# Turning a gate vector on VectorE before it is stored, and giving the two halves of a last tile a buffer each

## The chip, the core and the metric

The kernel runs on one core of a Trainium2 chip. Its engines work side by side, each through a queue of its own: TensorE (PE; its weight loads are listed apart as PEld), VectorE (DVE), ScalarE (ACT), GpSimd (POOL) and SyncE (SP), whose queue starts nearly all of this kernel's DMA transfers. They wait for each other by semaphores. The metric is the device time of one execution in microseconds (us); lower is better.

## What is computed

Two attention blocks work on the same x (2048 rows of 448 numbers), and a gate mixes them row by row:

```python
x = A_x
g = _sigmoid((x * gate_w).sum(-1, keepdims=True))
a = _A_ref(x, A_wqkv, A_wo)
b = _B_ref(x, B_wqkv, B_wo)
return g * a + (1 - g) * b
```

Both project x to queries, keys and values for 16 heads of 28 numbers, and multiply the heads' results by an output matrix. A lets each position see 8 positions, 2 apart (itself and those before it). B lets every position see all 2048 (softmax over the whole row). The change touches how `1 - g` is stored, and one of the projection's tiles.

## The kernel before, in words

Matmuls are done in split precision: an operand is rounded to a high part, the rest is kept as a low part, and three products are summed.

**Projection** (loop from line 476, about the first 254 us). There are 92 tiles: 28 for B's queries and keys, 16 for B's values, then 48 for A (16 each for queries, keys and values). From tile 10 on a tile is computed as two halves of the contraction, on the upper and the lower 64 rows of TensorE, into the two banks of a PSUM pair `PJ[n % 2]`. `add_halves` (line 380) then copies both banks to one SBUF tile `raw` in one ScalarE instruction (line 387), and GpSimd adds the two halves into a staging tile `ast` (line 388). Each staging tile takes two projected tiles and is then stored to DRAM by SyncE (line 401). Between the projection's matmuls run half matmuls of B's scores (line 148), of which VectorE takes the row maxima (line 170), four of them for every two tiles.

Tile 90, the last that goes through `PJ`, is copied otherwise: ScalarE copies one half (line 384) and VectorE the other (line 385), because the main stage needs that PSUM at once. Tile 91 is computed at the start of the main stage in another bank (`last_tile`, line 459) and stored from line 466.

**Buffers.** `raw`, `ast` and later the probability tiles `P` (written by the exponentials, line 1021), `ow` and `tw` all come from one pool, `pair`, with 8 buffers of 128x2x512 numbers. A tile that gets a buffer waits until everything that used it before is done, a store from it included. The main stage takes five `P` tiles from it with its first five exponentials and reuses these five to the end.

**Gate.** Two columns of the weights for A's queries give the gate's logits, which GpSimd gathers in `zt` (128 partitions x 16 columns; row 16 p + j of x stands in partition p, column j). At tile 64 ScalarE takes the exponentials, at tiles 66 and 68 VectorE the reciprocals: `g_t` holds g, `omg` holds 1 - g. At tile 70 SyncE stores `omg` to a DRAM vector `og_scr` (line 539), turned: column j, partition p goes to place 128 j + p. Sixteen small loads (line 938) bring it back in the main stage as `og`, in the layout in which B's sums stand. `omg` has another use before that: while it is still zero, it is the source of two stores that clear the margin before A's keys and values (line 515, at tile 16).

**Main stage** (from line 1031, to about 830 us). 16 units of 16 steps; a step has 12 score matmuls (line 1016), up to three matmuls of scores for the maxima of a later unit (line 148), two exponentials, and 8 matmuls with the values (line 982). A's part runs on GpSimd and VectorE meanwhile. The **output** product (line 862) follows.

The order of the work on each queue is the order of the program's lines as it is written out. On SyncE the gate store follows the staging store of tile 70 and stands ahead of the staging store of tile 71 and of the loads into `QP` (line 99, called from line 133). The maxima of a unit are turned (`max_turn`, line 198) and stored in four pieces of 32 columns (`max_store`, line 203) in the same way as the change does it for the gate.

Of the kernel before, what the change touches and what calls it, by code (L numbers as in the profile page):

```python
# [8 lines left out]
F32 = mybir.dt.float32  # L9
F32R = mybir.dt.float32r  # L10
AF = mybir.ActivationFunctionType
ALU = mybir.AluOpType
# [3 lines left out]
S, D, H, DH = 2048, 448, 16, 28  # L16
NB, NJ, NG = 4, 16, 4
# [8 lines left out]
def gated_mix_kernel(ctx: ExitStack, tc: tile.TileContext, xT, xn, gw, wA, wB, woAB, out):  # L26
    nc = tc.nc
# [12 lines left out]
    og_scr = dram.tile([S], F32, name="og_scr")  # L40
# [3 lines left out]
    cp = ctx.enter_context(tc.tile_pool(name="cp", bufs=1))  # L44
    sp = ctx.enter_context(tc.tile_pool(name="sp", bufs=2))
# [7 lines left out]
    PJ, PM = PS[0:2], PS[2:4]  # L53
# [8 lines left out]
    make_identity(nc, ident)  # L62
    V = cp.tile([128, NJ, H, 32], F32, name="V")
    g_t = cp.tile([128, NJ], F32, name="g_t")
    omg = cp.tile([128, NJ], F32, name="omg")
    zt = cp.tile([128, NJ], F32, name="zt")
    og = cp.tile([128, NB, 16], F32, name="og")

# [15 lines left out]
    def pair(name):  # L84
        return pp.tile([128, 2, 512], F32, tag="P", name=name)
# [124 lines left out]
    t0 = pair("t0")[:, 0, :]  # L210
    nc.vector.memset(t0, 0.0)  # L211
    nc.vector.memset(zt, 0.0)
    nc.vector.memset(omg, 0.0)

    def warm(n):
        for _ in range(n):
# [6 lines left out]
    if True:  # L223
# [30 lines left out]
        def split_x(nb):  # L254
            r, t = xst[:, nb, 0:3, :], xst[:, nb, 3, :]
            tail = xh[nb][:, 3, :]
            o, i = LOW[nb], HIGH[nb]
            for kt in (3, 0, 1, 2) if nb == 1 else range(4):
                if kt < 3:
                    split(xh[nb][:, kt, :], xl[nb][:, kt, :], r[:, kt, :])  # L260
                else:
                    nc.scalar.activation(tail[i], t[i], AF.Copy)
                    nc.vector.tensor_tensor(out=tail[o], in0=t[i], in1=tail[i].bitcast(F32), op=ALU.subtract)
# [3 lines left out]
        def load_w(wi, tails=(False, True)):  # L267
            src, cols = WSRC[wi]
            if wi not in wraw:
                wraw[wi] = raw3(), wp.tile([128, 450], F32, tag="wt", name="wt"), sum(c1 - c0 for c0, c1 in cols) + 2 * (wi == GATE)  # L270
            r, t, _ = wraw[wi]
            for tail in tails:
                o = 0
                for c0, c1 in cols:
                    e = o + c1 - c0
                    if tail:
                        both(t[:, o:e], src[384:448, c0:c1])
                    else:
                        nc.sync.dma_start(r[:, :, o:e], src[0:384, c0:c1].rearrange("(k p) c -> p k c", p=128))
                    o = e  # L280

                if wi == GATE:
                    if tail:
                        both(t[:, o:o + 2], gw[0:2, 384:448].rearrange("i p -> p i"))
                    else:
                        for kt in range(3):
                            nc.sync.dma_start(r[:, kt, o:o + 2],
                                              gw[0:2, 128 * kt:128 * kt + 128].rearrange("i p -> p i"))

        def split_w(wi, kts):  # L290
            if wi not in wsets:
                wsets[wi] = [wp.tile([128, 4, 450], F32R, tag=g, name=f"{g}{wi}") for g in ("wh", "wl")]
            wh, wl = wsets[wi]
            r, t, n = wraw[wi]
            for kt in kts:
                split(wh[:, kt, :n], wl[:, kt, :n], r[:, kt, :n] if kt < 3 else t[:, :n], nc.gpsimd)
# [24 lines left out]
        def project(n):  # L321
            if n == 0:
                for m, p in FIRST:
                    product(m, p, None, p == (0, 0, 0), p == (0, 1, 3))
            elif n > 1:
                for i, p in enumerate(ORDER):
                    product(n, p, None, i == 0, i == len(ORDER) - 1)
# [51 lines left out]

        def add_halves(n, dst, gate=None):  # L380
            raw = pair("raw")
            cols = D + 2 * (gate is not None)
            if n == len(tiles) - 2:
                nc.scalar.activation(raw[:, 0, 0:cols], PJ[n % 2][:, 0, 0:cols], AF.Copy)  # L384
                nc.vector.tensor_copy(raw[:, 1, 0:cols], PJ[n % 2][:, 1, 0:cols])  # L385
            else:
                nc.scalar.activation(raw[:, :, 0:cols], PJ[n % 2][:, :, 0:cols], AF.Copy)  # L387
            nc.gpsimd.tensor_tensor(out=dst, in0=raw[:, 0, 0:D].rearrange("p (c e) -> p c e", e=dst.shape[-1]),  # L388
                                    in1=raw[:, 1, 0:D].rearrange("p (c e) -> p c e", e=dst.shape[-1]), op=ALU.add)
            if gate is not None:  # L390
                nc.gpsimd.tensor_tensor(out=gate, in0=raw[:, 0, D:D + 1], in1=raw[:, 1, D:D + 1], op=ALU.add)

# [2 lines left out]
        def a_tile(n, i, j):  # L395
            k = j // 8
            if j % 2 == 0:
                stage[k] = pair("ast").rearrange("p a b -> p (a b)")[:, 0:896].rearrange("p (c j e) -> p c j e", c=8, j=2)
            add_halves(n, stage[k][:, :, j % 2, :], zt[:, j:j + 1] if tiles[n][0] == GATE else None)
            if j % 2 == 1:  # L400
                nc.sync.dma_start(a_own[i][:, :, j - 1:j + 1, :].rearrange("c p j e -> p c j e"), stage[k])
# [28 lines left out]
        r, t = xst[:, 0, 0:3, :], xst[:, 0, 3, :]  # L430
# [3 lines left out]
        for kt in range(3):  # L434
            if kt:
# [3 lines left out]
                                    op=ALU.subtract)  # L439
            nc.vector.tensor_tensor(out=wl0[:, kt, wa], in0=wr0[:, kt, 0:256], in1=wh0[:, kt, wa].bitcast(F32),  # L440
                                    op=ALU.subtract)
# [34 lines left out]
        for n, t in enumerate(tiles[:-1]):  # L476
            wi = t[0]
            for w in loads:
                if loads[w] == n:
                    load_w(w)  # L480
            for w in splits:
                i, k = (n - splits[w][0]) * splits[w][1], splits[w][1]
                if 0 <= i < 4:
                    split_w(w, range(i, i + k))
            if n in (3, 5):
                split_x((n + 1) // 2)
            if n < FULL:
                project(n)
            else:
                project_halves(n, [S1_START <= m < S1_START + 80 for m in (n, n + 1)])  # L490
            if t[1] == "qk":
                for m in {0: (), 1: (0, 1)}.get(n, (n,)):
                    qk_tile(m, *tiles[m][2:4])
            elif t[1] == "v":
                add_halves(n, V[:, t[2], :, 0:DH])
            else:
                a_tile(n, t[2], t[3])
            if n == 1:
                split_x(1)
            if n == 4:  # L500
                for t in QP[1]:
                    nc.scalar.activation(t, t0, AF.Copy)
            while fini and fini[0][0] <= n:
                fini.pop(0)[1]()
            if n == 2:
                load_w(1, (False,))
            if n == 3:
                load_qhi(0)
            if n in (3, 8):
                load_k(0, KH[0], qk_hi, slice(0, 1024) if n == 3 else slice(1024, S))  # L510
            if n == 3:
                load_w(1, (True,))
            if n == 16:
                for i in (1, 2):
                    nc.sync.dma_start(a_scr[i][:, 0:NJ, :].rearrange("c j e -> c (j e)").rearrange(
                        "c (a b) -> c a b", b=NJ), omg[0:8, None, :].to_broadcast([8, 56, NJ]))
            if n == 32:
                nc.gpsimd.memset(V[:, :, :, DH:], 1.0)
            if n == 22:
                load_k(1, KH[1], qk_hi)  # L520
            if n == 62:
                load_k(0, KL[0], qk_lo)
            if parts and parts[0][0] <= n:
                _, u, t = parts.pop(0)
                max_store(u, max_turn(t))
            if finished and n < len(tiles) - 3:
                u = finished.pop(0)
                parts.append((n + 3, u, max_parts(u)))
            if n == 64:
                gate = []  # L530
                for sgn, dst in ((-1.0, g_t), (1.0, omg)):
                    e = sp.tile([128, NJ], F32, name="ez")
                    nc.scalar.activation(e, zt, AF.Exp, scale=sgn)
                    nc.gpsimd.tensor_tensor(out=e, in0=e, in1=V[:, 0, :, DH], op=ALU.add)
                    gate.append((dst, e))
            if n in (66, 68):
                nc.vector.reciprocal(*gate.pop(0))
            if n == 70:
                nc.sync.dma_start(og_scr.rearrange("(j p) -> p j", j=NJ), omg)
            if n == 76:  # L540
                load_q(0)

# [186 lines left out]
    for c in range(8):  # L729
# [20 lines left out]
        n = 0  # L750
# [365 lines left out]
```

## Time and profile before

| | |
|---|---|
| three runs | 900.95, 901.16, 902.78 us (median 901.16) |
| profiled execution | 902.81 us, of which the span of the core's instructions is 901.0 us |
| TensorE busy | 893.7 us, 99% of the span |
| VectorE, ScalarE, GpSimd busy | 82%, 71%, 71% |
| mean granted TensorE clock | 0.998 of full speed |
| DMA | 104.51 MB, mean 116 GB/s |

Rows of a timeline have the start in us from the span's start, the duration, the engine, the line of the kernel, the operation, output <- inputs, shapes and a count of merged instructions; in brackets stands how long the engine was idle before, and what ended that. Rows of waits have the waiting engine, its instruction, what released it, the total, the count and the longest. A table of stretches has, for each stretch of the span, its length, the busy time of PE, PEld, DVE, ACT and POOL with the number of instructions, the granted TensorE clock, the DMA engines' busy share (over 1 where transfers overlap on an engine) and the GB/s. The ends of matmuls are modelled, so a busy TensorE is not always one at full speed.

### The profile page before, as it was taken

What the parts mean: (1) busy time and instruction counts of PE and PEld (TensorE: products, weight loads), DVE (VectorE), ACT (ScalarE), POOL (GpSimd) and SP (SyncE); (2) the same over time, 40 slices, a digit from 0 to 9 for tenths busy, and PEclk for the clock granted to TensorE, in tenths of its full rate; (3) what the DMA queues carried; (4) which work ended last, traced back from release to release, by engine and by line L of the source; (5) the groups of instructions that cost most, each with busy time, mean ns of one, the idle gap of its engine ahead of it and who ended that gap; (6) DMA issues with size and microseconds to landing.
All of it is one profiled execution on the core that took longest, in us unless ns stands there. A gap on an engine that the chain in (4) does not pass through costs nothing.

```text
span 901.0 us, 20505 instructions
## 1 busy us (share of the span) xinstructions
PE 893.7 (99%) x8311; PEld 534.3 (59%) x8311; DVE 739.9 (82%) x962; ACT 642.4 (71%) x765; POOL 638.5 (71%) x505
## 2 busy tenths in 40 slices
PE   9999999999999999999999999999999999999998
PEld 7889999998954444444444444444444444434997
DVE  6688999997979999999999999999999999832220
ACT  6456434343368888988988989889888898897220
POOL 1489846463449789999999999999999698501000
PEclk9999999999999999999999999999999999999999
DMA  8887403459373242225325342452130322347681
GB/s 267 276 260 192 144 12 84 138 141 95 100 227 107 88 130 53 62 60 147 85 52 143 88 111 47 105 131 73 51 63 20 94 43 56 96 90 199 184 270 52
DMA packets 115974, 104.51 MB, mean 116 GB/s; under 512 B 77176, under 2 KB 84216, under 8 KB 115096
## 3 DMA queue, kind: packets, MB, share of 16 engines
q1 hardware_dynamic: 115448, 102.42, 42.7%
q8 instruction: 65, 1.06, 0.5%
q10 hardware_dynamic: 432, 0.79, 0.2%
q14 instruction: 29, 0.24, 0.1%
HBM read 62.20 MB, written 40.96 MB: 114 GB/s over the span
## 4 chain that ended last, share of the span: by engine, by line
PE 99%; ACT 1%; issue 0%; DVE 0%; ACTq 0%
PE T L1016 31%; PE av L982 28%; PE r L319 15%; PE r L314 8%; PE T L862 8%; PE r L148 4%; PE T L148 4%; PE r L217 0%; ACT P L1021 0%; PE av L462 0%; ACT raw L387 0%; DVE raw L385 0%; ACT raw L384 0%; ACT onhi L919 0%; DVE t L211 0%
## 5 line engine op out<-in xcount | busy, mean ns | idle before, releaser
L1021 ACT ACTIVATE P<-T 128x1024 f32<-128x1024 f32 x512 | 496.9, 1023 | 60.5 <-PE T L1016 58.4
L154 DVE TENSOR_REDUCE MX<-T 128x1 f32<-128x512 f32 x470 | 442.1, 954 | 32.9 <-PE T L148 15.7
L982 PE MATMUL av<-P,V 128*32 128x512 f32 x2048 | 272.7, 605 | 0.0
L1016 PEld LDWEIGHTS T<-QH,KH 30*128 30x128 f32 x1024 | 92.1, 181 | 230.1 <-ACT P L1021 196.5
L148 PE MATMUL T<-KH,QP 28*128 28x512 f32 x704 | 220.0, 456 | 0.4 <-DVE raw L385 0.4
L170 DVE TENSOR_REDUCE MX<-r 128x2 f32<-128x1024 f32 x160 | 192.7, 1221 | 24.2 <-PE r L148 21.6
L1016 PE MATMUL T<-QH,KH 30*128 30x512 f32 x1024 | 212.0, 489 | 0.2 <-ACT P L1021 0.2
L1016 PE MATMUL T<-QH,KL 28*128 28x512 f32 x1024 | 186.8, 395 | 0.0
L1016 PE MATMUL T<-QL,KH 28*128 28x512 f32 x1024 | 184.6, 392 | 0.0
L637 POOL TENSOR_TENSOR prod<-qt,kt 128x896 f32<-128x896 f32 x64 | 135.3, 2115 | 6.4 <-DMA kt<-a_scr 6.3
L387 ACT ACTIVATE raw<-r 128x896 f32<-128x896 f32 (+1 forms) x62 | 57.0, 920 | 98.4 <-PE r L319 91.9
L148 PE MATMUL r<-KH,QP 64*128 64x512 f32 x320 | 108.3, 394 | 1.1 <-issue 1.1
L698 POOL TENSOR_TENSOR oat<-oat,prod 128x896 f32<-128x896 f32 x48 | 101.2, 2108 | 2.0
L148 PEld LDWEIGHTS T<-KH,QP 28*128 28x128 f32 x704 | 86.0, 181 | 27.5 <-ACT P L1021 19.1
L388 POOL TENSOR_TENSOR ast<-raw 128x448 f32<-128x448 f32 x47 | 54.2, 1155 | 60.6 <-ACT raw L387 54.4
L319 PE MATMUL r<-wh,xh 64*128 64x448 f32 (+1 forms) x504 | 96.2, 367 | 0.5 <-ACT raw L387 0.5
L693 POOL TENSOR_TENSOR prod<-vt,L 128x896 f32<-128x896 f32 x56 | 95.3, 1702 | 0.2
L1016 PEld LDWEIGHTS T<-QL,KH 28*128 28x128 f32 x1024 | 94.5, 185 | 0.0
L1016 PEld LDWEIGHTS T<-QH,KL 28*128 28x128 f32 x1024 | 93.3, 183 | 0.2
L982 PEld LDWEIGHTS av<-P,V 128*32 128x32 f32 x2048 | 40.3, 107 | 77.6 <-issue 65.3
L319 PE MATMUL r<-wl,xh 64*128 64x448 f32 (+1 forms) x441 | 75.7, 368 | 0.0
L319 PEld LDWEIGHTS r<-wh,xh 64*128 64x128 f32 x504 | 74.6, 187 | 1.2 <-ACT raw L387 0.8
(121 smaller groups left out, 1129.1 us busy)
## 6 DMA issues: line engine op xcount, KB each, us to landing
a_scr<-ast SPq DMA_DIRECT2D x24, 448.0 KB
qk_hi<-qkh SPq DMA_DIRECT2D x24, 256.0 KB
qk_lo<-qkh SPq DMA_DIRECT2D x24, 256.0 KB
rbc<-rs SPq DMA_DIRECT2D x64, 64.0 KB
QP<-qk_hi SPq DMA_DIRECT2D x64, 56.0 KB
KL<-qk_lo SPq DMA_DIRECT2D x16, 224.0 KB
QH<-qk_hi SPq DMA_DIRECT2D x64, 56.0 KB
QL<-qk_lo SPq DMA_DIRECT2D x64, 56.0 KB
```

Of the source, the lines that this page charges most:

```text
L148: nc.tensor.matmul(bank, qhis[u][h % 2][r, 128 * qs:128 * qs + 128], KH[u // NB % 3][r, 512 * kc:512 * kc + 512], start=True, stop=True)
L154: i = nc.vector.tensor_reduce(MX[:, n % NMX:n % NMX + k], bank, axis=X, op=ALU.max)
L170: nc.vector.tensor_reduce(m, PM[k], axis=X, op=ALU.max)
L314: nc.tensor.matmul(bank, ws[c][rows, k, t[4]:t[4] + 128], x, start=first, stop=last)
L319: nc.tensor.matmul(bank[:, 0:cols], x, ws[c][rows, k, 0:cols], start=first, stop=last)
L637: nc.gpsimd.tensor_tensor(out=p, in0=qt[c], in1=kvt["k", c % 2][:, HALO - DIL * w:HALO - DIL * w + NJ, :], op=ALU.mult)
L693: nc.gpsimd.tensor_tensor(out=dst.rearrange("p j (h d) -> p j h d", d=DH), in0=kvt["v", c % 2][:, HALO - DIL * w:HALO - DIL * w + NJ, :].r ...
L698: nc.gpsimd.tensor_tensor(out=ows[c % 2][:, :, 0:56] if w == W - 1 else oat[c], in0=oat[c], in1=oat[c, w], op=ALU.add)
L862: writes(bank, nc.tensor.matmul(bank[:, :D], src, wo[c][k], start=(first and k == ks[0] and i == 0), stop=(last and k == ks[-1] and i == 2)))
L982: nc.tensor.matmul(av[32 * h:32 * h + 32, :], V[:, kt, 4 * g + h, :], tiles_[h], start=(kt == 0), stop=(kt == NJ - 1), skip_group_check=True)
L1016: nc.tensor.matmul(bank[a], (KH[g % 3], KH[g % 3], KL[g % 2])[t][r, ks], (qh, ql, qh)[t][r, :], start=(t == 0), stop=(t == 2))
L1021: e = nc.scalar.activation(p, one if a == "2" else mine, AF.Exp, scale=SCALE).ins
```

## The change

`omg` becomes the first 16 columns of a wider tile `omt` (128x32), which is cleared whole. At tile 70 VectorE turns `omt` in blocks of 32x32 into a new tile `r`, and SyncE stores 16 rows of each of its four groups of 32 partitions: four transfers with rows of 32 numbers (128 bytes) that lie together in DRAM, in place of one transfer of single numbers. And the second half of tile 90 goes to a buffer of its own, a further tile from `pair`; GpSimd's sum then reads the two.

```diff
-    omg = cp.tile([128, NJ], F32, name="omg")
+    omt = cp.tile([128, 32], F32, name="omt")
+    omg = omt[:, 0:NJ]
...
-    nc.vector.memset(omg, 0.0)
+    nc.vector.memset(omt, 0.0)
...
         def add_halves(n, dst, gate=None):
             raw = pair("raw")
+            other = raw[:, 1, :]
             cols = D + 2 * (gate is not None)
             if n == len(tiles) - 2:
                 nc.scalar.activation(raw[:, 0, 0:cols], PJ[n % 2][:, 0, 0:cols], AF.Copy)
-                nc.vector.tensor_copy(raw[:, 1, 0:cols], PJ[n % 2][:, 1, 0:cols])
+                other = pair("raw")[:, 1, :]
+                nc.vector.tensor_copy(other[:, 0:cols], PJ[n % 2][:, 1, 0:cols])
...
-                                    in1=raw[:, 1, 0:D].rearrange("p (c e) -> p c e", e=dst.shape[-1]), op=ALU.add)
+                                    in1=other[:, 0:D].rearrange("p (c e) -> p c e", e=dst.shape[-1]), op=ALU.add)
...
             if n == 70:
-                nc.sync.dma_start(og_scr.rearrange("(j p) -> p j", j=NJ), omg)
+                r = sp.tile([128, 32], F32, name="omr")
+                nc.vector.transpose(r, omt)
+                for a in range(4):
+                    nc.sync.dma_start(og_scr.rearrange("(j p) -> j p", j=NJ)[:, 32 * a:32 * a + 32],
+                                      r[32 * a:32 * a + NJ, :])
```

## The prediction

> **What bounds the kernel now.** I read the page first: busy shares and the chain that ended last.
>
> ```profile
> span 901.0 us, 20505 instructions
> PE 893.7 (99%) x8311; PEld 534.3 (59%) x8311; DVE 739.9 (82%) x962; ACT 642.4 (71%) x765; POOL 638.5 (71%) x505
> PE 99%; ACT 1%; issue 0%; DVE 0%; ACTq 0%
> ```
>
> TensorE carries the chain almost alone. So an edit on DVE, ACT or the DMA queues is worth only what it takes out of TensorE's own stream: idle time, and time in which it runs slower than elsewhere. The waits of TensorE show the idle time, 3.7 us in all:
>
> ```profile
> PE r L217 <- DVE omg L213: 1.5, 1, 1.5
> PE r L148 <- issue: 1.1, 1, 1.1
> PE r L319 <- ACT raw L387: 0.5, 1, 0.5
> PE T L148 <- DVE raw L385: 0.4, 1, 0.4
> ```
>
> The last row names the copy that the change splits off. The second and third I looked up in the timeline, and they lie together, at 213 to 215 us, soon after the gate store. A table of stretches around that store, with its last three columns (granted clock, DMA share, GB/s), shows more than the waits do:
>
> ```profile
> 204.00:214.00 10.00, 8.95 (x84) 8.54 (x83) 7.12 (x7) 2.14 (x4) 3.64 (x4) 1.00 1.36 27
> 214.00:216.00 2.00, 1.53 (x11) 0.98 (x9) 1.26 (x2) 1.58 (x2) 0.59 (x1) 0.84 1.44 178
> 216.00:218.00 2.00, 2.00 (x14) 1.77 (x12) 2.00 (x3) 0.14 (x1) 1.65 (x2) 0.50 0.90 243
> 218.00:220.00 2.00, 2.00 (x20) 1.84 (x18) 1.00 (x2) 0.03 (x1) 0.00 (x0) 0.81 0.84 229
> 222.00:253.00 31.00, 31.00 (x300) 30.29 (x297) 27.55 (x23) 11.04 (x12) 13.67 (x13) 1.00 0.37 99
> ```
>
> From 204 to 214 us the DMA engines are full (share 1.36) and move 27 GB/s; in the quiet stage after 222 us they move 99 GB/s at a share of 0.37. At the end of that jam TensorE falters, and then runs at half clock. SyncE's queue tells what went in just before:
>
> ```profile
> 172.41 1.72 SPq L205 DMA_DIRECT2D nm<-nms  x4
> ...
> 200.41 0.53 SPq L539 DMA_DIRECT2D og_scr<-omg  x1
> 202.62 0.36 SPq L401 DMA_DIRECT2D a_scr<-ast  x1
> 203.62 6.23 SPq L99 DMA_DIRECT2D QP<-qk_hi  x4
> ```
>
> The gate store L539 puts 2048 numbers of 4 bytes where no two neighbours of a row lie together: 2048 pieces. Staging stores (L401) go on through the quiet stage after 222 us without a jam, so I put the jam down to L539.
>
> What it costs is read from ScalarE's copy L387, one per projected tile:
>
> ```profile
> 197.78 0.92 ACT L387 ACTIVATE raw<-r 128x896 f32<-128x896 f32 x1 [1.62 <-PE r L319]
> ...
> 208.29 0.92 ACT L387 ACTIVATE raw<-r 128x896 f32<-128x896 f32 x1 [1.32 <-PE r L319]
> 214.42 1.73 ACT L387 ACTIVATE raw<-r 128x896 f32<-128x896 f32 x2 [5.21 <-PE r L148]
> ...
> 222.48 0.92 ACT L387 ACTIVATE raw<-r 128x896 f32<-128x896 f32 x1 [1.59 <-PE r L319]
> ...
> 232.88 0.92 ACT L387 ACTIVATE raw<-r 128x896 f32<-128x896 f32 x1 [1.60 <-PE r L319]
> ```
>
> Four tiles before the jam take 208.29 - 197.78 = 10.51 us, four after it 232.88 - 222.48 = 10.40, the four across it 14.19. The jam costs 3.68 to 3.79 us; I take 3.74. The granted clock explains part: 2 us at 0.84, 0.50 and 0.81 lose 0.32 + 1.00 + 0.38 = 1.70 us. The other 2.04 are the two gaps (1.05 and 0.47 us) and weak filling around them.
>
> **The change, part by part.**
>
> *Gate store.* Removed: L539, one issue of 0.53 us and its 2048 pieces. Added: one VectorE transpose, four issues and 64 pieces of 128 bytes. Both have a twin in this kernel, the maxima's turn L200 and store L205, of the same 128x32 shape and 128-byte rows:
>
> ```profile
> L200 DVE STREAM_TRANSPOSE nms<-nmt x16: 199/202/219, 88.3 to 786.8; 128x32 f32<-128x32 f32 x16
> 172.40:174.40 2.00, 2.00 (x23) 2.00 (x21) 1.92 (x2) 0.21 (x2) 1.16 (x1) 1.00 0.64 181
> 197.31 2.36 DVE L170 TENSOR_REDUCE MX<-r 128x2 f32<-128x1024 f32 x2 [0.27 <-PE r L148]
> ```
>
> The transpose takes 0.20 us among the maxima near 198.5 us, where VectorE idles 0.27 us (197.31) and so holds it. Without it a maximum would be 0.20 late, and so would the next score half. Behind SyncE's new wait stand the four issues and the staging store at 202.62; the transpose is done before SyncE reaches it at 200.41, and four issues of L205's kind (1.72) end at 202.13, so nobody is moved. The twin's stretch (172.40 to 174.40) has TensorE full at clock 1.00: the new pieces cost TensorE nothing there. Their bounds: 0 below; above, the whole 3.74 if 128 bytes jam as 4 do. At the old jam's rate, 14 us (200.41 to 214.42) for 2048 pieces, 64 would take 0.44 us of DMA, off TensorE's path. I take 0, by the twin. The Trainium skill ("DMA: Bandwidth & Descriptors", Specifications) speaks against the edit: pieces under 512 bytes cause a read-modify-write, and 128 is still under. By that the new store stays of the slow kind and part of the 3.74 would be left; the twin's row disagrees, and the sum goes by it.
>
> How much of 3.74 leaves? The profile does not show the jam as releaser of TensorE: the rows name issue and ACT, and ACT in turn names TensorE. So the gain is bounded by 0 and 3.79. I take 3.74, because full DMA engines, falter and clock follow each other within one jam and nowhere else.
>
> *Memset L213* grows from 16 to 32 columns:
>
> ```profile
> 1.37 0.07 DVE L213 MEMSET omg<- 128x16 f32 x1
> 5.28 0.52 PEld L314 LDWEIGHTS r<-xh,wh 128*128 128x128 f32 x2 [0.34 <-ACT wh L437]
> ```
>
> At most another 0.07 us before the warm-up matmuls; the first real weight load waits 0.34 us for ScalarE. Cost 0.
>
> *Two buffers for tile 90.* The halves are copied by ScalarE (L384) and VectorE (L385), today one after the other:
>
> ```profile
> 253.24 0.54 ACT L384 ACTIVATE raw<-r 128x448 f32<-128x448 f32 x1 [1.16 <-PE r L319]
> 253.66 0.39 PE L1016 MATMUL T<-QH,KL 28*128 28x512 f32 x1
> 253.82 0.62 DVE L385 COPY raw<-r 128x448 f32<-128x448 f32 x1 [2.07 <-ACT raw L384]
> 254.50 0.50 PE L148 MATMUL T<-KH,QP 28*128 28x512 f32 x2 [0.44 <-DVE raw L385]
> 254.52 1.15 POOL L388 TENSOR_TENSOR ast<-raw 128x448 f32<-128x448 f32 x1 [1.15 <-DVE raw L385]
> ```
>
> VectorE has been idle for 2.07 us and starts 0.04 us after ScalarE ends. With its own buffer it starts at 253.24 and ends at 253.86, before TensorE's previous matmul ends (253.66 + 0.39 = 254.05). Gain 0.44 us, TensorE's whole idle time; it is 0 if the wait comes from the PSUM tile that both read. GpSimd's sum and its store start 0.58 us earlier and nobody waits for them. Later stages are TensorE's own, so the shift reaches the end.
>
> The added buffer is the ninth claim on eight, and moves the first five probability tiles by one. Their rows:
>
> ```profile
> 258.39 1.94 ACT L1021 ACTIVATE P<-T 128x1024 f32<-128x1024 f32 x2 [0.36 <-PE T L1016]
> 258.52 0.38 SPq L466 DMA_DIRECT2D a_scr<-ast  x1
> 260.58 1.94 ACT L1021 ACTIVATE P<-T 128x1024 f32<-128x1024 f32 x2 [0.26 <-PE T L1016]
> 261.90 0.32 SPq L630 DMA_DIRECT2D vt<-a_scr  x1
> SPq L630 <- DMA a_scr<-ast: 0.9, 1, 0.9
> ```
>
> A buffer whose store is in flight would hold an exponential. If a buffer that came free earlier is taken first, as I assume, the plain copies' buffers go first and no store is met: cost 0. Bounds 0 to 3.51, below.
>
> *Sum.* The profiled execution took 902.81 us (span 901.0 and 1.81 around it): 902.81 - 3.74 - 0.44 = **898.6**. It is 1.65 above the median 901.16, about the 1.70 us that the half clock cost. If the median run has the gaps but not the half clock, 901.16 - 2.04 - 0.44 = 898.7: the same place.
>
> **Rivals.**
>
> *The stall is no part of ordinary runs.* What the DMA jam holds may be only the recording of this execution, or the store only delays transfers that nobody needs yet. For it: no engine's wait names L539, and the median lies 1.65 lower. Against: granted clock and tile spacing agree with it to 0.05 us. Then only the copy counts: 901.16 - 0.44 = 900.7.
>
> *The half clock stays.* The clock falls after gaps of 1.05 and 0.47 us only, so another cause could lie behind it. Then 902.81 - 2.04 - 0.44 = 900.3. The Trainium skill ("TensorE: Matmul & The Clock Gate", HAM oscillation) has the clock drop after idle stretches over about 3.4 us, which these gaps are not; by that rule this would be the outcome. The rows speak for the jam: elsewhere in these stretches the clock is 1.00.
>
> *Buffers in strict turn.* Probability tile 2 gets the staging buffer of tile 88, tile 4 that of 89. A staging store lands 261.90 - 258.52 = 3.38 us after its issue. Tile 88's goes at 254.52 + 1.15 - 0.58 = 255.09 and lands at 258.47; the exponential due at 258.39 - 0.44 = 257.95 waits 0.52. Tile 89's then goes at 258.60 and lands at 261.98, and the exponential due at 260.66 waits 1.32. 898.6 + 1.84 = 900.5.
>
> *Slower: one exponential behind the last staging store.* If tile 2 gets tile 89's buffer, it is due at 257.95 and the store lands at 258.08 + 3.38 = 261.46: 3.51 us, long enough to cost the half clock again, 1.70. 898.6 + 5.2 = 903.8. It decides from 2.5 us on, where it outweighs the gain against the median. Against it: today no exponential waits for a transfer, and that buffer is the last to come free.
>
> **How the numbers follow.** Forecast 0.58. Stall no part of ordinary runs 0.14, half clock stays 0.05, strict turn 0.08: all near 900.5, inside 0.2% of 901.16 (1.8 us, about what a measurement of this kernel can tell from no change). Slower 0.15. So faster 0.58, same 0.27, slower 0.15. The forecast's own range is 897.0 (901.16 - 3.74 - 0.44, the whole stall in the median run) to 899.3; the stated one reaches to the middle cases, 897.0 to 901.1, and leaves out the 0.15.
>
> **What would show it.** Right: no stretch after the gate store with a DMA share over 1 and under 50 GB/s; clock 1.00 from 200 to 253 us; tile copies 2.6 us apart throughout; VectorE's copy starting with ScalarE's; no wait of TensorE for it; no exponential that waits for a transfer. Wrong: the tile spacing still breaks a few microseconds after the four stores (128 bytes jam too), or it is smooth and the time hardly moves (the stall was not in the median run), or ScalarE idles at 258 to 262 us.

## The result and the profile after

The changed kernel takes 899.39 us (median of 18 runs, 898.89 to 900.20) beside 901.14 us (18 runs, 899.41 to 904.03) for the kernel before: a ratio of 0.9977, 95% interval 0.9969 to 0.9984. That is 1.75 us faster by the medians, about a fifth of a per cent; the ratio is lower, like that of the means (899.38 and 901.50), because the kernel before has more long executions. (One execution of the kernel before, at 1038 us and a mean clock of 0.75, is left out of every comparison below.) The forecast was 898.6, in a range of 897.0 to 901.1. The profiled execution took 899.97 us, 2.84 less than the one of before.

The page: TensorE is still busy for 99% of the span and carries 96% of the chain that ended last.

```profile
span 898.2 us, 20509 instructions
PE 891.3 (99%) x8311; PEld 532.8 (59%) x8311; DVE 739.9 (82%) x963; ACT 642.6 (72%) x765; POOL 639.0 (71%) x505
PE 96%; DMA 1%; SPq 1%; ACT 1%; DVE 0%; issue 0%; ACTq 0%
```

The waits of TensorE (what released it, total us, count, longest). The two rows behind the old gate store (issue 1.1, ACT raw 0.5) are gone. The wait for VectorE's half of tile 90, which the split was to remove, is there as before.

```profile
PE r L218 <- DVE omt L214: 1.5, 1, 1.5
PE T L1023 <- DVE MX L155: 0.5, 1, 0.5
PE T L149 <- DVE raw L388: 0.5, 1, 0.5
PE r L315 <- ACT xh L232: 0.3, 1, 0.3
PE T L1023 <- ACT P L1028: 0.2, 1, 0.2
```

The stretches around the gate store, in the same columns as before. DMA share 1.36 at 27 GB/s has become 0.40 at 112 GB/s, TensorE has 99 matmuls in the 10 us instead of 84, and the granted clock is 1.00 throughout.

```profile
200.40:204.00 3.60, 3.60 (x38) 3.60 (x37) 3.33 (x4) 1.81 (x2) 1.16 (x1) 1.00 0.55 143
204.00:214.00 10.00, 10.00 (x99) 10.00 (x97) 9.32 (x9) 3.52 (x7) 4.81 (x5) 1.00 0.40 112
214.00:216.00 2.00, 2.00 (x23) 2.00 (x21) 1.94 (x4) 0.49 (x1) 1.15 (x1) 1.00 0.82 234
216.00:218.00 2.00, 2.00 (x22) 2.00 (x20) 1.98 (x2) 0.92 (x1) 0.68 (x1) 1.00 0.19 57
```

The timeline: SyncE's queue, ScalarE's copies of tile 74 and of tile 78, and at the end the copy of tile 90.

```profile
200.49 2.33 SPq L545 DMA_DIRECT2D og_scr<-omr  x4
202.91 0.38 SPq L404 DMA_DIRECT2D a_scr<-ast  x1
203.69 2.63 SPq L100 DMA_DIRECT2D QP<-qk_hi  x4
...
208.36 0.92 ACT L390 ACTIVATE raw<-r 128x896 f32<-128x896 f32 x1 [1.32 <-PE r L320]
218.78 0.92 ACT L390 ACTIVATE raw<-r 128x896 f32<-128x896 f32 x1 [1.59 <-PE r L320]
...
249.53 0.55 ACT L386 ACTIVATE raw<-r 128x448 f32<-128x448 f32 x1 [1.14 <-PE r L320]
250.10 0.62 DVE L388 COPY raw<-r 128x448 f32<-128x448 f32 x1 [2.08 <-ACT raw L386]
250.78 0.50 PE L149 MATMUL T<-KH,QP 28*128 28x512 f32 x2 [0.46 <-DVE raw L388]
```

The four tiles across the old jam now take 218.78 - 208.36 = 10.42 us, where they took 14.19: 3.77 us less. VectorE's copy of tile 90 still starts when ScalarE's ends (249.53 + 0.55), though the two write different buffers.

Of the 3.77 us, 2.84 are left at the end of this execution. Matched matmul by matmul against the execution before, some 0.6 are given back near 594 us: VectorE waits 0.91 us there for a small load, and the maxima behind it are what TensorE waits for in the second row of the waits.

```profile
593.40 0.25 DVE L903 RECIPROCAL finv<-fsum 128x16 f32<-128x16 f32 x1 [0.91 <-DMA fsum<-rs]
```

The change does not touch that load. The loss appeared in some of the kernels below and not in others, with and without either edit, so I read it as chance of the DMA's timing, which no run here tests. The other 0.3 has no wait of its own.

### The profile page after: what moved, and what is told of

It is laid out like the page before. It is cut to its first block, busy times and chain, and to the rows that moved or that the text cites. A ratio compares the mean times of both kernels' runs of the same rounds, so it can differ in the third digit from the quotient of the medians.

```text
span 898.2 us, 20509 instructions
## 1 busy us (share of the span) xinstructions
PE 891.3 (99%) x8311; PEld 532.8 (59%) x8311; DVE 739.9 (82%) x963; ACT 642.6 (72%) x765; POOL 639.0 (71%) x505
## 4 chain that ended last, share of the span: by engine, by line
PE 96%; DMA 1%; SPq 1%; ACT 1%; DVE 0%; issue 0%; ACTq 0%
PE T L1023 30%; PE av L989 27%; PE r L320 15%; PE T L869 8%; PE r L315 7%; PE r L149 4%; PE T L149 4%; DMA V<-in_xT 1%; SPq L717 1%; SPq L100 1%; ACT P L1028 0%; PE av L465 0%; DMA fsum<-rs 0%; DVE MX L155 0%; SPq L419 0%
## 5 line engine op out<-in xcount | busy, mean ns | idle before, releaser
L1028 ACT ACTIVATE P<-T 128x1024 f32<-128x1024 f32 x512 | 497.0, 1024 | 61.0 <-PE T L1023 59.0
L149 PE MATMUL r<-KH,QP 64*128 64x512 f32 x320 | 115.0, 391 | 0.0
L320 PE MATMUL r<-wh,xh 64*128 64x448 f32 (+1 forms) x504 | 100.0, 363 | 0.0
L320 PE MATMUL r<-wl,xh 64*128 64x448 f32 (+1 forms) x441 | 79.4, 365 | 0.0
L320 PEld LDWEIGHTS r<-wh,xh 64*128 64x128 f32 x504 | 77.9, 185 | 0.1
```

The source lines that it names most:

```text
L149: nc.tensor.matmul(bank, qhis[u][h % 2][r, 128 * qs:128 * qs + 128], KH[u // NB % 3][r, 512 * kc:512 * kc + 512], start=True, stop=True)
L320: nc.tensor.matmul(bank[:, 0:cols], x, ws[c][rows, k, 0:cols], start=first, stop=last)
L1028: e = nc.scalar.activation(p, one if a == "2" else mine, AF.Exp, scale=SCALE).ins
```

## The experiments

Unless it is said otherwise, a time is a median beside the kernel before on the same chip, which took 900.7 to 901.3 us.

### One edit at a time

`e1_gate_only` is the kernel before with the turned gate store alone:

```diff
-    omg = cp.tile([128, NJ], F32, name="omg")
+    omt = cp.tile([128, 32], F32, name="omt")
+    omg = omt[:, 0:NJ]
...
-                nc.sync.dma_start(og_scr.rearrange("(j p) -> p j", j=NJ), omg)
+                r = sp.tile([128, 32], F32, name="omr")
+                nc.vector.transpose(r, omt)
+                for a in range(4):
+                    nc.sync.dma_start(og_scr.rearrange("(j p) -> j p", j=NJ)[:, 32 * a:32 * a + 32],
+                                      r[32 * a:32 * a + NJ, :])
```

> Only the gate part of the change. Theory (the gate store carries the whole gain): ratio to before 0.998, the same as for the whole change, tile copies 2.6 us apart across 208 to 222 us, clock 1.00 there, TensorE's 0.4 us wait for VectorE's copy of tile 90 still there. Rival (the copy part has its 0.44 us share): the ratio lies 0.0005 nearer to 1 than the whole change's.

Measured: 899.06 us, ratio 0.9978 (0.9969 to 0.9987). That is the whole gain of the change. The stretch after the store:

```profile
204.00:214.00 10.00, 10.00 (x99) 10.00 (x98) 9.31 (x10) 3.77 (x6) 4.62 (x5) 1.00 0.39 108
```

`e2_split_only` is the kernel before with the second buffer for tile 90 alone:

```diff
...
-                nc.vector.tensor_copy(raw[:, 1, 0:cols], PJ[n % 2][:, 1, 0:cols])
+                other = pair("raw")[:, 1, :]
+                nc.vector.tensor_copy(other[:, 0:cols], PJ[n % 2][:, 1, 0:cols])
...
```

> Only the two buffers for tile 90. Theory (VectorE waits because both copies read one PSUM tile, and a second buffer does not touch that): VectorE's copy still starts 0.03 to 0.04 us after ScalarE's ends, TensorE's wait stays at 0.4 to 0.5 us, ratio 1.000 with the jam after the 4-byte store still in the trace. Rival (the shared buffer was the cause): VectorE's copy starts with ScalarE's, TensorE does not wait, ratio 0.9995.

Measured: 900.66 us, ratio 0.9992 (0.9982 to 1.0001): no gain that can be told from none. First its timeline at tile 90, then its stretches after the gate store, where the jam is as it was.

```profile
251.57 0.62 DVE L387 COPY raw<-r 128x448 f32<-128x448 f32 x1 [2.07 <-ACT raw L385]
252.25 0.50 PE L148 MATMUL T<-KH,QP 28*128 28x512 f32 x2 [0.44 <-DVE raw L387]
```

```profile
204.00:214.00 10.00, 9.81 (x89) 8.98 (x85) 7.26 (x8) 2.79 (x5) 3.64 (x4) 1.00 1.38 33
214.00:216.00 2.00, 1.58 (x12) 1.14 (x14) 2.00 (x2) 1.08 (x2) 1.44 (x2) 1.00 1.06 259
216.00:218.00 2.00, 2.00 (x22) 1.84 (x22) 2.00 (x4) 0.26 (x1) 0.84 (x1) 1.00 1.15 327
```

The granted clock stays at 1.00 here: the jam came without the half clock.

`e3_split_free` is the changed kernel with the order between the two copies taken away. Both read one PSUM tile, in different banks; the declared independence touches nothing else.

```diff
-                nc.scalar.activation(raw[:, 0, 0:cols], PJ[n % 2][:, 0, 0:cols], AF.Copy)
+                first = nc.scalar.activation(raw[:, 0, 0:cols], PJ[n % 2][:, 0, 0:cols], AF.Copy).ins
                 other = pair("raw")[:, 1, :]
-                nc.vector.tensor_copy(other[:, 0:cols], PJ[n % 2][:, 1, 0:cols])
+                second = nc.vector.tensor_copy(other[:, 0:cols], PJ[n % 2][:, 1, 0:cols]).ins
+                tc.declare_no_dep(second, first, reason="other bank, other buffer")
```

> The changed kernel, with the dependence of VectorE's copy of tile 90 on ScalarE's copy declared away (they read different PSUM banks and write different buffers). Theory: VectorE's copy starts at the end of tile 90's matmuls together with ScalarE's, TensorE's wait of 0.46 us is gone, and the first score matmuls of the main stage come 0.4 us earlier against the changed kernel; ratio to before 0.9975, 0.0005 below the whole change's. Rival (something else holds TensorE there): VectorE's copy is early but TensorE waits on and nothing moves.

```profile
249.29 0.54 ACT L386 ACTIVATE raw<-r 128x448 f32<-128x448 f32 x1 [1.16 <-PE r L320]
249.38 0.62 DVE L388 COPY raw<-r 128x448 f32<-128x448 f32 x1 [1.60 <-PE r L320]
```

The copies now run side by side, each released by TensorE, and TensorE's wait for `raw` is gone. Matched against `e1_gate_only`, the first matmuls of the main stage come 0.34 us earlier in the trace. The time is 899.04 us, ratio 0.9974 (0.9964 to 0.9984): 0.02 us under `e1_gate_only`, which a measurement of this width cannot tell from 0.34 or from nothing. It is the fastest form that was run with both edits and nothing added, but within the intervals it is no different from the change itself.

`e4_before_again` is the kernel before, unchanged, profiled once more.

> The kernel before, unchanged, profiled once more. If the jam after the gate store is a property of the program, the four tiles across it again take 14 us in place of 10.5, and TensorE's program transfer, due at about 208 us, comes after 214 us. If the size of the stall is a matter of chance, the four tiles take anything from 10.5 to 16 us, in step with this run's time between 899.4 and 904.

Profiled once more, it took 900.4 us. Its copies (tiles 74, 75 and 76, 77, 78) and its stretches:

```profile
208.12 0.92 ACT L388 ACTIVATE raw<-r 128x896 f32<-128x896 f32 x1 [1.31 <-PE r L320]
213.46 1.73 ACT L388 ACTIVATE raw<-r 128x896 f32<-128x896 f32 x2 [4.41 <-remote]
217.49 0.92 ACT L388 ACTIVATE raw<-r 128x896 f32<-128x896 f32 x1 [2.31 <-PE r L320]
220.01 0.92 ACT L388 ACTIVATE raw<-r 128x896 f32<-128x896 f32 x1 [1.59 <-PE r L320]
```

```profile
204.00:214.00 10.00, 9.60 (x88) 8.85 (x84) 7.42 (x8) 2.69 (x5) 3.52 (x4) 1.00 1.32 38
214.00:216.00 2.00, 1.66 (x17) 1.38 (x18) 2.00 (x4) 1.19 (x2) 1.55 (x2) 1.00 1.03 259
216.00:218.00 2.00, 2.00 (x22) 1.89 (x20) 2.00 (x3) 0.51 (x1) 0.72 (x1) 1.00 1.00 287
```

The same jam, again without the half clock. The four tiles take 220.01 - 208.12 = 11.89 us, 1.47 over the 10.42 without a jam; in `e2_split_only` it was 11.99, 1.57 over. So the 3.74 us of the prediction were a jam of about 1.5 us and, on top of it, the loss of clock and what goes with it (about 2.2 us), which these two executions do not have.

How often it happens, the clocks on record tell. Of 92 executions of the kernel before that ran beside the experiments, 15 have a mean granted clock of 0.996 to 0.998, as the profiled one of the prediction has (0.998), and took 902.7 to 905.0 us. The other 77, at 0.999 or 1.000, took 899.8 to 902.3 us. So about one execution in six paid for the clock as well. None of the 117 executions of kernels with the new gate store fell below 0.999, and none of the 12 of `e2_split_only`, which are too few to tell.

### What in the jam costs the time

The jam was put at another place, where the change had left the DMA engines quiet: the changed kernel with a further store of 2048 numbers of 4 bytes to a place in DRAM that nobody reads, at tile 76, 78 or 82. What the kernel computes stays the same.

```diff
+    extra = dram.tile([S], F32, name="extra")
...
+            if n == 76:
+                nc.sync.dma_start(extra.rearrange("(j p) -> p j", j=NJ), omg)
```

One explanation to be tested was that TensorE's program is itself fetched by DMA, 16 KB about every 13 us (queue 8, of the kind "instruction"; that these are TensorE's is an assumption), and starves in the jam; the places differ in when the next fetch is due.

> The changed kernel plus an extra store of the gate vector in 2048 pieces of 4 bytes, side by side in DRAM, to a place that nobody reads, issued at tile 76 (about 216 us). Theory A (the jam of these writes delays TensorE's program transfer, which comes about every 13 us, and TensorE starves): the transfer due at 220.5 us comes 4 us into the jam and is held some 9 us; four tiles across it take 4 us more or longer. Theory B (the jam delays the signals by which TensorE releases VectorE and ScalarE, whatever the program transfer does): 1.4 us more as in the second look at the kernel before, or 3 to 4 with a half clock.

> The same extra store at tile 78 (about 221 us), just behind a program transfer; the next one is due at 234.5 us, when the jam of 13 to 14 us ends. Theory A: no stall, tiles stay 2.6 us apart, time as the changed kernel's within 0.3 us. Theory B: 1.4 us more, the same as at tiles 70 and 76.

> The same extra store at tile 82 (about 232 us), 2 to 3 us ahead of the program transfer due at 234.5 us. Theory A: the transfer is held about 11 us, the largest stall of the three, 5 us or more. Theory B: 1.4 us more again (3 to 4 with a half clock).

| extra store | time (us) | ratio, interval | delay in the trace (us) |
|---|---|---|---|
| tile 76 | 899.98 | 0.9986, 0.9975 to 0.9997 | 1.12 |
| tile 78 | 900.09 | 0.9984, 0.9975 to 0.9993 | 0.68 |
| tile 82 | 900.02 | 0.9987, 0.9978 to 0.9997 | 0.73 |

The delay is by how much the way from the copy of tile 74 to that of tile 90 is longer than the 249.53 - 208.36 = 41.17 us of the changed kernel. (The expectations further down have 0.9 us for tile 82; counted in this way it is 0.73.) In time, every place costs about the same: 1.08 to 1.19 us over the 898.90 of `x82_spread` below, which ran beside them. That is the pattern of the other explanation (the jam itself costs, wherever it lies), though it had 1.4 us of delay. The program fetch falls as the common cause: at tile 78 none was due inside the jam (they came at 220.6 and 236.0 us), and still ScalarE's copy was late. At tile 76 the fetch was held as forecast (to 230.0 us), without the 4 us of delay that were to follow from it. First tile 76, where the profile names a staging store as releaser, then tile 78, where it names TensorE:

```profile
228.93 0.92 ACT L391 ACTIVATE raw<-r 128x896 f32<-128x896 f32 x1 [1.24 <-PE r L321]
233.92 1.73 ACT L391 ACTIVATE raw<-r 128x896 f32<-128x896 f32 x2 [4.07 <-DMA a_scr<-ast]
```

```profile
229.10 0.92 ACT L391 ACTIVATE raw<-r 128x896 f32<-128x896 f32 x1 [1.59 <-PE r L321]
233.53 1.73 ACT L391 ACTIVATE raw<-r 128x896 f32<-128x896 f32 x2 [3.51 <-PE r L150]
```

### What makes the jam

`x82_spread` has the same 2048 pieces at tile 82, 512 bytes apart:

```diff
-    extra = dram.tile([S], F32, name="extra")
+    extra = dram.tile([S, 128], F32, name="extra")
...
-                nc.sync.dma_start(extra.rearrange("(j p) -> p j", j=NJ), omg)
+                nc.sync.dma_start(extra[:, 0].rearrange("(j p) -> p j", j=NJ), omg)
```

> As the extra store at tile 82, the same 2048 pieces of 4 bytes, but 512 bytes apart in DRAM. If the number of small pieces makes the jam: DMA share over 1 and under 50 GB/s for 10 us or more, and the same stall as with packed pieces. If it is their lying side by side (writes into the same few kilobytes that wait for each other): the jam is gone or under 4 us, and the time is the changed kernel's.

Measured: 898.90 us, ratio 0.9976 (0.9965 to 0.9986), delay 0.00. The number of pieces and their size are as before, so these two alone do not make a jam.

The next two lie between: `x82_64b` puts the pieces 64 bytes apart (`[S, 16]`), `x82_half` stores half of them, side by side (`[:, 0:NJ // 2]` of both sides of the store).

> The changed kernel plus the extra store of 2048 numbers of 4 bytes at tile 82 (nobody reads it), its pieces 64 bytes apart, so that 8 of them share 512 bytes. If pieces hold each other when they lie in the same 512 bytes, this jams as the packed store did: DMA share over 1 below 40 GB/s for about 12 us after 231 us, one ScalarE copy about 0.9 us late, time about 900.0. If they hold each other only as next neighbours (within 64 bytes), there is no jam: copies 2.6 us apart, time 898.9 to 899.4, as with pieces 512 bytes apart.

> The same extra store with 1024 numbers of 4 bytes instead of 2048, side by side in 4 KB. If the jam is a queue of pieces each of which takes its time, it lasts half as long (some 6 to 7 us instead of 12 to 14), and ScalarE's copy, which was late by 0.9 us behind 2048 pieces, is late by 0.5 us or not at all: time 899.2 to 899.8. If the jam's length is set by something else than the number of pieces, it stays at 12 us and the time at about 900.0.

`x82_64b` took 899.54 us, ratio 0.9970 (0.9956 to 0.9984), all copies 2.6 us apart. `x82_half` is a miss: 901.16 us, ratio 0.9990 (0.9977 to 1.0002), and a delay of 1.9 us in its trace, though it has half the pieces; 899.2 to 899.8 was expected if the pieces count, about 900.0 if they do not.

That led to another idea: the length is set by how many pieces share 64 bytes (16, when they lie side by side), since these are written one after the other. `x82_16b` has 2048 pieces 16 bytes apart (`[S, 4]`), `x82_256pieces` only 256 side by side (`[:, 0:2]`).

> The changed kernel plus the extra store of 2048 numbers of 4 bytes at tile 82 (nobody reads it), its pieces 16 bytes apart: 4 of them share 64 bytes, where 16 do when they lie side by side. In the runs so far 2048 and 1024 pieces side by side jammed equally long, some 10 us, and pieces 64 bytes apart not at all. Theory C: pieces that share 64 bytes are written one after the other, about 0.6 us each (10 us / 16), all stretches of 64 bytes beside each other. Then this jams for about 4 x 0.6 = 2.5 us, ScalarE's copies stay 2.6 us apart or miss by at most 0.3 us, and the time is 898.9 to 899.5. Rival: any two pieces within 64 bytes bring the whole jam: 10 us, copy late by 0.9 to 1.9 us, time 900.0 to 901.2.

> The same extra store with only 256 numbers of 4 bytes, side by side in 1 KB (16 to each 64 bytes, as before). Theory C: the jam is as long as with 2048 pieces, about 10 us after 233 us with staging pieces of 448 bytes that take hundreds of ns, a ScalarE copy 0.9 to 1.9 us late, time 900.0 to 901.2. Rival, by the number of pieces (an eighth of them): at most 1.3 us of jam, no late copy, time 898.9 to 899.5.

`x82_16b` took 899.12 us, ratio 0.9981 (0.9972 to 0.9990); `x82_256pieces` 899.13, ratio 0.9983 (0.9973 to 0.9992); in neither is a copy late. The GB/s rows of the DMA view from 230 to 250 us, in 40 slices of half a microsecond, show the length of each jam. In this order: 2048 side by side, 1024, 256, then 2048 at 16, 64 and 512 bytes.

```profile
GB/s 0 0 0 98 310 228 270 18 7 187 58 13 11 11 13 17 24 16 31 14 26 14 20 18 17 25 30 74 202 227 240 230 234 234 233 231 233 119 13 5
```

```profile
GB/s 0 0 0 0 221 294 271 135 4 165 252 7 21 12 5 6 8 5 12 8 12 9 9 13 22 15 22 33 47 172 245 237 232 226 241 233 235 220 89 5
```

```profile
GB/s 0 0 0 0 207 298 287 128 0 157 292 181 8 1 4 6 12 27 20 5 22 19 4 15 54 32 250 259 237 186 212 266 254 189 92 11 0 0 0 0
```

```profile
GB/s 0 0 0 0 140 307 220 251 8 8 204 79 68 65 44 65 85 194 139 9 0 0 0 0 0 204 306 280 127 0 117 308 296 229 0 0 0 0 0 0
```

```profile
GB/s 0 0 0 193 297 216 214 7 21 208 102 132 134 193 152 15 0 0 0 0 0 0 0 0 255 305 271 87 0 171 306 289 184 0 0 0 0 0 0 0
```

```profile
GB/s 0 0 0 253 286 237 146 7 53 190 141 95 121 209 136 12 0 0 0 0 0 0 0 14 305 303 257 39 0 235 306 274 135 0 0 0 0 0 0 0
```

In each row the staging stores move at over 200 GB/s, the 4-byte pieces follow (the dip to under 60 near 234 us), and then the transfer behind them either crawls or does not. With 2048 side by side it crawls for 8 us (16 slices, at most 31 GB/s), with 1024 for 9 (18 slices, at most 47), with 256 still for 7 (14 slices, at most 54). With 16 bytes between them it moves at 44 to 85 GB/s for 3 us, and with 64 or 512 bytes there is no crawl (102 and 95 GB/s in the lowest slice). So the length does not follow the number of pieces; it follows how close together they lie. That is the idea's pattern, but only roughly its numbers: it had 10 us for 256 pieces and 2.5 us for 16 bytes between them, and 7 and 3 were measured. The time of the 256 pieces came as the rival by number had it (898.9 to 899.5). What exactly must be shared is not shown: with the distance the whole stretch grew too, from 1, 4 and 8 KB (7, 9 and 8 us) to 32, 128 and 1024 KB (3, 0 and 0 us), and 256 pieces 16 bytes apart, which would tell the two apart, were not run.

Single transfers in the trace show where the time goes: in `x82_half` the records of the 4-byte pieces, 7 to 8 ns each, end by 234.4 us, and the pieces of 448 bytes behind them then take 0.4 to 1.1 us each (means by microsecond, 236 to 243 us), where they take 25 ns before. So the staging store *behind* the small pieces waits. But the small store is not done either when its pieces seem to be: its landings are recorded from 241.8 to 243.9 us, those of `x82_spread` from 236.0 to 236.8.

What was not expected is the last step: 256 pieces jam the DMA for 7 us and ScalarE's copies are on time, 1024 jam it for 9 and ScalarE is 1.9 us late. The delay begins in the last microseconds of a jam, and its size is not in proportion to it. One wait there can be read. The staging store behind the small pieces lands last at 244.77 us with 256 of them and at 246.27 with 2048, and the sum on GpSimd that waits for it comes at its usual pace in the first case and late in the second, where the profile names that store:

```profile
245.65 1.15 POOL L392 TENSOR_TENSOR ast<-raw 128x448 f32<-128x448 f32 x1 [1.42 <-ACT raw L391]
```

```profile
246.41 1.15 POOL L392 TENSOR_TENSOR ast<-raw 128x448 f32<-128x448 f32 x1 [2.50 <-DMA a_scr<-ast]
```

A jam that ends before the store is waited for costs GpSimd nothing, and one that ends 1.5 us later holds it. ScalarE's first late copy, at 244.74 us with 2048 pieces, comes before that landing and is not explained by it.

## Why the prediction was right, and where not

**The place was right.** The jam comes from the gate store: with the store changed alone it is gone (`e1_gate_only`), with the rest changed alone it stays (`e2_split_only`), and a store of the same form put elsewhere brings it back.

**The new store costs nothing: right.** The pieces of 128 bytes leave TensorE full at clock 1.00, as their twin's did. The four issues took 2.33 us instead of the forecast 1.72, so the next staging store left SyncE at 202.91 instead of 202.62, and nobody waited for it. The rule of the Trainium skill ("DMA: Bandwidth & Descriptors", Specifications), by which pieces under 512 bytes are of the slow kind, would have left part of the jam; here 128 bytes did not jam, and neither did 4 bytes at 64 bytes from each other. That 512 bytes is where the trouble begins is not what these runs show.

**The size of the jam in the median was mis-sized.** In the profiled execution the copies gave 3.77 us, where 3.74 was forecast. But the second path of the sum, which took the two gaps out of the median (901.16 - 2.04), set the jam of an ordinary run too high by about 0.5: it is 1.47 and 1.57 us in the other two traces of the kernel with the old store. With that, and nothing for the split, the median would be 899.6 to 899.7, and 899.39 was measured. The median of before was 1.65 us under its profiled execution, and the prediction read that rightly as the half clock: the executions at 0.999 and above lie at 902.3 us and below. What it did not have was a second profile to size the rest. That its two ways to the sum met at 898.6 and 898.7 was chance. The first, from the profiled execution, holds the whole jam of 3.74 rightly, but 899.97 was measured there: 0.44 is the split that gained nothing, and 0.9 was lost later on. The second was too low by 0.44 for the split and by about 0.5 for the jam. The stated range, 4.1 us wide, took both in.

**The half clock** went with the jam, so the rival in which it stays fell. But two executions had the jam and kept the clock at 1.00, and so, by their mean clock, did 77 of 92. What decides whether it falls is open.

**The split gained nothing: this step failed.** The 0.44 us rested on the two copies sharing a buffer. They also share the PSUM tile that both read, and the program orders two readers of one tile even in different banks; the prediction named that case at 0 and did not choose it. `e2_split_only` shows the wait unchanged, and `e3_split_free` shows it gone when that order is lifted. The row that the prediction quotes, VectorE's copy released by ScalarE's, fits both cases: a shared buffer written in two halves was no better reason for it than a shared source.

**Buffers: right.** The exponentials that take the first probability tiles wait for TensorE or for nothing shown, never for a transfer, so both rivals with a staging store in the way fell:

```profile
254.73 1.94 ACT L1028 ACTIVATE P<-T 128x1024 f32<-128x1024 f32 x2 [0.42 <-PE T L1023]
256.87 1.94 ACT L1028 ACTIVATE P<-T 128x1024 f32<-128x1024 f32 x2 [0.19 <-issue]
259.17 1.94 ACT L1028 ACTIVATE P<-T 128x1024 f32<-128x1024 f32 x2 [0.36 <-PE T L1023]
```

**The stall is no part of ordinary runs:** this rival fell for the runs on record. `e1_gate_only` is 1.75 us faster in the median, and each extra packed store takes 1.1 to 1.2 us of that away. But the record has the span and the clock of every execution, so none of them ran without being recorded; that the recording has a part in the stall is not excluded.

**Still open** is what holds the engines near the end of a jam. ScalarE's and VectorE's rows name TensorE, a staging store or no engine of this core ("remote"), by the run, and TensorE's own names only its issue. The records of that stretch are thinner than elsewhere: of the 16 landings that a store normally leaves, the old gate store left 7, 6 and 5 in three traces. So most releasers there cannot be trusted. Two fit their own records: GpSimd's above, and that of ScalarE in `x76_packed`. There the staging store that the row names left SyncE only at 230.53 us, since SyncE stood until the extra store's last landing (227.51), and has all its 16 landings; the last, at 233.85, comes 0.07 us before the copy. In that run it is SyncE's queue, held by the small store, that reaches ScalarE. The Trainium skill ("NOTIFIC — the notification-queue block", 7.1 Overflow) says that the inner part of the block that writes trace records holds back what produces them rather than lose a record inside it. No run here shows that. If such records had to pass the same jam, they could hold the engines; the missing landings show that some were lost all the same, and an execution that writes no records was not tried.

## What to carry to other kernels

Read a store by where its pieces fall in DRAM, not only by their size: small numbers from many partitions that land side by side can hold up the transfers queued behind them for 7 to 9 us, as here, and one 32x32 turn on VectorE (0.20 us here) or some space between them takes that away. Before a cost that is read from one profiled execution goes into a forecast of the median, profile the same kernel again: here the cost was 3.7 us in one and 1.5 in the next two. And before a second buffer is added to free a copy, look for everything that the two instructions share, the source too.

## What the hardware showed that was not expected

- 256 pieces of 4 bytes side by side (1 KB in all) held the DMA engines under 55 GB/s for 7 us, nearly as long as 2048 pieces (8 us); 2048 pieces 64 bytes apart did not hold them.
- Where the DMA engines crawled for 7 us ScalarE's copies came on time; where they crawled for 8 and 9 us, ScalarE's copies were 0.7 and 1.9 us late.
- The same jam cost the TensorE clock in one execution (0.84, 0.50 and 0.81 granted over 6 us) and left it at 1.00 in two others. By the mean clock, 15 of 92 executions of the kernel before had the fall.
